# A new order of work between the set-up and the first feed-forward group of a two-layer S4 and SwiGLU network, the weights' high halves all cast on ScalarE, the norms' mean factor on GpSimd

## The chip, the core and the metric

One core of one Trainium2 chip runs the whole program. The metric is device time in microseconds (us), from the start of the execution to its end. The core has five instruction streams that each run strictly in order and wait for each other through semaphores: TensorE (PE in the profile), VectorE (DVE), ScalarE (ACT), GpSimd (POOL) and SyncE (SP, which here issues most of the DMAs).

## The reference

The input `u` is 1 x 2048 x 512 in fp32. Two layers follow one another, each an S4 convolution and a SwiGLU feed-forward step, both on a layer norm and both with a residual:

```python
def _A_ref(u, A_re, A_im, B_re, B_im, C_re, C_im, log_dt, Dskip):
    ...                                   # K: 512 kernels of length L, sums of 128 modes exp(dt*A*l)
    Yf = Uf * Kf[None, :, :, :]           # products of spectra, padded to 2L
    y = irfft(...)[..., :L]
    return y + u * Dskip
def _B_ref(x, w_gate, w_up, w_down):      # 512 -> 1376 -> 512
    return (_silu(x @ w_gate) * (x @ w_up)) @ w_down
x = A_u
for _ in range(2):                        # the same weights in both layers
    x = x + _A_ref(_layernorm(x), ...)
    x = x + _B_ref(_layernorm(x), w_gate, w_up, w_down)
```

## The kernel before, in words

**Blocks and groups.** The 2048 tokens are cut into four blocks of 512. Layer and block go in the order `SEQ` = (0,0), (0,1), (0,2), (1,0), (0,3), (1,1), (1,2), (1,3). A block first has its convolution (`ssm`, two halves of 256 channels, `ssm_half`) and then its feed-forward step in two groups of 256 tokens. The sixteen groups are counted here from 0, so group 2 is the first group of block (0,1) and group 4 the first of (0,2).

**The convolution** works on blocks of frequencies. In a half, four steps multiply the spectrum of the input by that of the kernel on VectorE (`yk`, a row of 128x1024 elements, L812, with `t` and L815 where there is an earlier block to add), take real and imaginary parts apart (L820, L821), and combine steps (L767, L768, L833 to L845). TensorE turns them back (`pi`, L784), and VectorE adds them to the residual (`xg` or `xf`, L793). The forward transform of the next input is `pf` on TensorE (L277).

**A feed-forward group** takes its layer norm in `ffn_norm`: `row_stats` sums rows on ScalarE (L223, L225, L226), GpSimd makes the inverse deviation by `pow` (L227), VectorE the factor of the mean (L228). Then, for each of two chunks of 128 tokens, ScalarE scales (L883) and casts to fp16 (L884), VectorE forms the low half `nn` (L885), and SyncE transposes both into `nhl2` (L887). TensorE then does `pgu`: a remainder of 48 small matmuls (L899 to L901; the first 24 read only the first chunk), and five turns of 48 (L930 to L933). Each turn ends in ScalarE's silu (`sg`, L936), VectorE's product (`sg`, L937), ScalarE's `hh` (L938) and VectorE's `hl` (L939). There are two buffers of `pgu` and two of `sg`. Last come 66 matmuls `py` (L946 to L948), and two VectorE rows (L953), one for each chunk, add them to the residual. The matmuls of a chunk end only with the last six of the 66.

**The set-up** makes the kernels' spectra in eight pieces ("lags", `pk`) and writes them out. **The transition** runs from the last lags to the first feed-forward group. There its order is written by hand for TensorE, VectorE, ScalarE and GpSimd, in generators advanced by `take(generator, n)`: `conv[0]` and `conv[1]` are the two halves of the first block, `first_parts` (L589, L590) completes the spectra `w0r` that the second half multiplies by, `odd` and `rest` are later spectra (`pw` L544 on TensorE, `wos` L607 and L608 on ScalarE, L609 on VectorE, a store by SyncE), `norm` is the first norm (statistics L207 to L213, `nn` L864, transposed on TensorE as `pt`, high half L869 on ScalarE, low half L871 on VectorE), `block1` the convolution of block (0,1), `last` a direct transform. `split(hi, lo, load)` takes the next steps of casting the weights to two fp16 halves: high halves of gate and up columns (ScalarE L675, the very first on VectorE L673), of w_down (ScalarE L700), low halves on VectorE (L680, L703), loads by SyncE (L668 for columns, L694 for w_down).

**After the transition** a list scheduler orders every engine with a timeline of its own, from the same program. Engines still run in the order so fixed.

Of the kernel before, what the change touches and what calls it, by code (L numbers as in the profile page):

```python
# [15 lines left out]
AF = mybir.ActivationFunctionType  # L16
OP = mybir.AluOpType
# [58 lines left out]
def kernel(ctx, tc, x, a_re, a_im, b_re, b_im, c_re, c_im, log_dt, d_skip,  # L76
# [139 lines left out]
    def row_stats(src, rows, scale, tag, junk):  # L216

        mv = tl([P, 4, 2], "mv", tag)
        rs = tl([P, 8], "rs", tag)
        nb = rs[:, 4:]  # L220
        c = 1.0 / (math.sqrt(D) * scale)
        for r in range(rows):
            A.activation(junk(r), src[:, r], AF.Identity, scale=-c / D, accum_out=mv[:, r, 0:1])  # L223
        for r in range(rows):
            A.activation(junk(r), src[:, r], AF.Square, scale=c, bias=mv[:, r, 0:1], accum_out=mv[:, r, 1:2])  # L225
        A.activation(mv[:, :rows, 1], mv[:, :rows, 1], AF.Identity, bias=epst[:, 0:1] if scale == 1.0 else epst[:, 1:2])  # L226
        G.tensor_tensor(rs[:, :rows], mv[:, :rows, 1], mhalf[:, :rows], OP.pow)  # L227
        V.scalar_tensor_tensor(nb[:, :rows], mv[:, :rows, 0], 1.0 / c, rs[:, :rows], OP.mult, OP.mult)  # L228
# [284 lines left out]
    def skip(ch, kt, eng):  # L513

        k = kt[0:1, :, 0]
        eng.tensor_tensor(k, k, dsk[:, ch * DC:(ch + 1) * DC].rearrange("p (g d) -> p g d", g=4), OP.add)
# [136 lines left out]
    def split_weights():  # L653


        cb = F // 4
        tags = iter(("bt", 0, 1, 2, "bt", 0, 1, 2, "n", "xf", "bt"))

        def columns(j, wi, src):
            fs = slice(j * cb, (j + 1) * cb)  # L660
            sc = sc6[:, wi:wi + 1]
            at = []

            def load():
                tag = next(tags)
                st = tl([P, 4, cb], "st2", tag) if isinstance(tag, str) else \
                    wsl[3].bitcast(F32)[:, 4 * cb * tag:4 * cb * (tag + 1)].rearrange("p (k f) -> p k f", k=4)
                nc.sync.dma_start(st, src[:, fs].rearrange("(k p) f -> p k f", p=P))  # L668
                at.append(st)

            def hi():
                if j == 0 and wi == 0:
                    V.tensor_scalar(wgu(wi, 0, 0, 4)[:, :, fs], at[0], sc, None, OP.mult)  # L673
                else:
                    A.activation(wgu(wi, 0, 0, 4)[:, :, fs], at[0], AF.Copy, scale=sc)  # L675

            def lo():
                n = 2 if wi == 0 else 4
                for k in range(0, 4, n):
                    V.scalar_tensor_tensor(wgu(wi, k, 1, n)[:, :, fs], at[0][:, k:k + n], sc,  # L680
                                           wgu(wi, 0, 0, 4)[:, k:k + n, fs], OP.mult, OP.subtract)
            return load, hi, lo

        def rows4(f0):
            n = min(4, F // P - f0)
            at = []

            def part(fc):
                rows = min(P, F - fc * P)
                sc = sc6[:rows, 2:3]  # L690

                def load():
                    st = tl([P, min(4, FT - f0), D], "st3", next(tags))
                    nc.sync.dma_start(st[:, :n], w_down[f0 * P:(f0 + n) * P].rearrange("(k p) d -> p k d", p=P))  # L694
                    if f0 + n < FT and n < 4:
                        nc.sync.dma_start(st[:F % P, n], w_down[(f0 + n) * P:])
                    at.append(st)

                def hi():
                    A.activation(wd(fc, 0)[:rows], at[0][:rows, fc - f0], AF.Copy, scale=sc)  # L700

                def lo():
                    V.scalar_tensor_tensor(wd(fc, 1)[:rows], at[0][:rows, fc - f0], sc, wd(fc, 0)[:rows],  # L703
                                           OP.mult, OP.subtract)
# [270 lines left out]
    with tc.manual_schedule(engines={mybir.EngineType.Activation, mybir.EngineType.DVE, mybir.EngineType.PE, mybir.EngineType.Pool}):  # L975
# [221 lines left out]
        take(tail["sp"], 2)  # L1197
        spread_pe(ks, kts[1])
        skip(c, kts[1], G)
        take(conv[0], 1)  # L1200
        while tops:
            tops.pop(0)()
        scales()
        split(1, 0)
        first_parts(c, 0)
        take(conv[0], 1)
        split(1, 1)
        split(0, 0, 1)
        first_parts(c, 2)
        split(1, 0)  # L1210
        take(conv[0], 1)
        first_parts(c - 1, 1)
        split(1, 0)
        take(last, 2)
        take(conv[1], 1)
        first_parts(c - 1, 3)
        take(conv[1], 1)
        split(0, 1)
        split(0, 0, 1)
        take(conv[0], 1)  # L1220
        take(conv[1], 1)
        split(1, 1)
        split(0, 0, 1)
        take(conv[1], 1)
        split(0, 1)
        split(0, 0, 1)
        take(odd, 2)
        take(conv[1], 1)
        direct_size()
        block1 = ssm(0, 1)  # L1230
        take(norm, 1)
        take(rest, 2)
        take(odd, 1)
        take(odd, 2)
        take(norm, 1)
        take(block1, 1)
        take(rest, 1)
        split(1, 0)
        take(odd, 1)
        take(norm, 1)  # L1240
        split(0, 1)
        take(rest, 3)
# [64 lines left out]
```

## Time and profile before

| | us |
|---|---|
| three runs: median (lowest to highest) | 1091.86 (1090.23 to 1092.86) |
| the profiled execution: its time, and its span | 1091.58, 1089.4 |
| PE busy in the span | 1026.5 (94%) |
| DVE busy | 969.3 (89%) |
| ACT busy | 547.4 (50%) |
| POOL busy | 109.6 (10%) |
| mean granted TensorE clock | 0.986 |

The time is the span and 2.2 us around it. Busy shares are means over stages with different limits, so the prediction reads them stage by stage. A row of the timeline gives the start, the length, engine, line and operation, the tile written and those read, and in brackets the idle time of the engine just before it and what ended it.

### The profile page before, as it was taken

Reading aid. Unit: us, or ns where it says so; the run is one execution under the profiler, and the core shown is the slowest. Engines: PE = TensorE matmul, PEld = TensorE weight load, DVE = VectorE, ACT = ScalarE, POOL = GpSimd, SP = SyncE. Lnnn points to the kernel's source line nnn. Section 1 sums busy time; section 2 is a strip of 40 time slices with the busy share of each in tenths; the row PEclk is TensorE's granted clock in tenths of the full one; section 3 lists DMA queues with packets and bytes.
Section 4 is the critical chain, followed back from the end, with each engine's and each line's share of the span. In section 5 each row is a group of like instructions: output and inputs, shape, how many; then the busy total and the mean of one; then the engine's idle time right before and its main releaser. Section 6 shows DMA issues by size and latency. Waiting matters only on the chain.

```text
span 1089.4 us, 22811 instructions
## 1 busy us (share of the span) xinstructions
PE 1026.5 (94%) x9302; PEld 810.9 (74%) x9302; DVE 969.3 (89%) x1405; ACT 547.4 (50%) x1093; POOL 109.6 (10%) x163
## 2 busy tenths in 40 slices
PE   1989999998779999999999999999999999999998
PEld 1868888887677777686779676786867687686775
DVE  8999999998999999999999989999998999993221
ACT  6989998953367162466462253533425432134211
POOL 1112222220002010012010001201100000000000
PEclk9989999998989999999999999999999999999999
DMA  5366777768765356342444553443545245312000
GB/s 212 108 180 167 173 166 179 187 181 272 234 182 172 120 145 215 105 141 68 131 117 133 158 160 130 119 136 100 166 126 180 59 127 147 109 61 63 2 25 20
DMA packets 125003, 149.23 MB, mean 137 GB/s; under 512 B 50897, under 2 KB 75985, under 8 KB 124130
## 3 DMA queue, kind: packets, MB, share of 16 engines
q1 hardware_dynamic: 112994, 122.27, 36.8%
q0 software_dynamic: 11904, 25.50, 10.0%
q8 instruction: 73, 1.20, 0.5%
q14 instruction: 32, 0.26, 0.1%
HBM read 97.66 MB, written 33.82 MB: 121 GB/s over the span
## 4 chain that ended last, share of the span: by engine, by line
PE 27%; DVE 27%; issue 11%; DMA 5%; ACT 3%; POOL 1%; SPq 0%; DVEq 0%; POOLq 0%; ACTq 0%
PE pgu L930 5%; PE pgu L931 5%; PE pgu L933 5%; DVE t L812 4%; DVE yk L815 4%; PE py L948 3%; PE py L946 3%; PE py L947 3%; DVE yk L812 3%; PE pi L784 2%; DVE sg L937 2%; DVE hl L939 2%; DMA n<-xdr 1%; DVE yl L232 1%; DMA mix<-nn 1%
## 5 line engine op out<-in xcount | busy, mean ns | idle before, releaser
L930 PE MATMUL pgu<-mix,wsl 128*128 128x256 f16 x1280 | 298.6, 273 | 5.4 <-DVE sg L937 2.1
L931 PE MATMUL pgu<-mix,wsl 128*128 128x256 f16 x1280 | 298.4, 273 | 0.0
L933 PE MATMUL pgu<-mix,wsl 128*128 128x256 f16 x1280 | 194.8, 273 | 0.0
L931 PEld LDWEIGHTS <-wsl 128*128 128x128 f16 x1280 | 125.2, 98 | 22.5 <-issue 6.7
L933 PEld LDWEIGHTS <-wsl 128*128 128x128 f16 x1280 | 125.2, 98 | 18.4 <-issue 3.8
L930 PEld LDWEIGHTS <-wsl 128*128 128x128 f16 x1280 | 125.2, 98 | 16.4 <-issue 1.2
L946 PE MATMUL py<-wsl,hh 128*128 128x512 f16 (+1 forms) x352 | 134.2, 381 | 0.1
L948 PE MATMUL py<-wsl,hl 128*128 128x512 f16 (+1 forms) x352 | 133.5, 381 | 0.1
L947 PE MATMUL py<-wsl,hh 128*128 128x512 f16 x320 | 121.8, 381 | 0.0
L815 DVE TENSOR_TENSOR yk<-yk,t 128x1024 f32<-128x1024 f32 x96 | 116.9, 1218 | 0.5
L812 DVE TENSOR_TENSOR t<-uu,w 128x1024 f32<-128x1024 f32 x96 | 117.0, 1218 | 0.3
L938 ACT ACTIVATE hh<-sg 128x512 f16<-128x512 f32 x80 | 50.1, 627 | 114.0 <-DVE sg L937 114.0
L544 PE MATMUL pw<-kt,ek 128*128 128x256 f32 (+1 forms) x384 | 93.2, 381 | 0.0
L937 DVE SCALAR_TENSOR_TENSOR sg<-pgu,sc,sg 128x512 f32<-128x512 f32 x80 | 59.6, 745 | 37.7 <-ACT sg L936 37.6
L936 ACT ACTIVATE sg<-pgu,sc 128x512 f32<-128x512 f32 x80 | 54.2, 678 | 70.7 <-PE pgu L933 66.9
L544 PEld LDWEIGHTS pw<-kt,ek 128*128 128x128 f32 x384 | 74.8, 199 | 8.8
L939 DVE TENSOR_TENSOR hl<-sg,hh 128x512 f16<-128x512 f32 x80 | 54.8, 685 | 15.3 <-ACT hh L938 15.3
L227 POOL TENSOR_TENSOR rs<-mv,mhalf 128x2 f32<-128x2 f32 (+1 forms) x21 | 33.6, 1598 | 336.3 <-ACT mv L226 296.3
L509 PE MATMUL pk<-re,g 128*32 128x64 f32 x1024 | 65.0, 317 | 2.2 <-DMA g<-g 1.9
L948 PEld LDWEIGHTS <-hl 128*128 128x128 f16 (+1 forms) x352 | 34.4, 98 | 39.2 <-issue 0.8
L947 PEld LDWEIGHTS <-hh 128*128 128x128 f16 (+1 forms) x352 | 34.6, 98 | 38.4 <-issue 0.8
L510 PE MATMUL pk<-im,g 128*32 128x64 f32 x1024 | 63.1, 301 | 0.0
(265 smaller groups left out, 2010.1 us busy)
## 6 DMA issues: line engine op xcount, KB each, us to landing
uu<-udr SPq DMA_DIRECT2D x96, 256.0 KB, 3.0
w<-wdr SPq DMA_DIRECT2D x96, 256.0 KB, 2.8
g<-g POOLq DMA_DIRECT2D x6, 1024.0 KB, 9.2
udr<-fu POOLq DMA_DIRECT2D x22, 256.0 KB, 2.7
udr<-u SPq DMA_DIRECT2D x16, 256.0 KB, 3.3
n<-xdr SPq DMA_DIRECT2D x4, 1024.0 KB, 6.4
kdr<-ks SPq DMA_DIRECT2D x6, 512.0 KB, 2.9
kt<-kdr SPq DMA_DIRECT2D x24, 128.0 KB, 3.0
```

The lines of the kernel that those rows point to most:

```text
L509: PE.matmul(o, lhsT=g[:, 0, :, d], rhs=re[:, 0:64, d], start=True, stop=False, tile_position=(0, 32 * grp))
L544: PE.matmul(pw[:, i], lhsT=e, rhs=kt[:, :, c + 4 * k0:4 * k1:4, :].rearrange("p g k d -> p k g d"), start=c == 0, stop=c == 3)
L812: V.tensor_tensor(t, uu.unsqueeze(2).to_broadcast([P, NQ, 2, 2, DC]), w.unsqueeze(3).to_broadcast([P, NQ, 2, 2, DC]), OP.mult)
L815: V.tensor_tensor(yk, yk, t, OP.add)
L930: PE.matmul(o, lhsT=wgu(wi, k, 0)[:, fs], rhs=nh[:, k], start=k == 0, stop=False)
L931: PE.matmul(o, lhsT=wgu(wi, k, 1)[:, fs], rhs=nh[:, k], start=False, stop=False)
L933: PE.matmul(o, lhsT=wgu(wi, k, 0)[:, fs], rhs=nlo[:, k], start=False, stop=k == 3)
L937: V.scalar_tensor_tensor(sg, pgu[:, 1], sc6[:, 4:5], sg, OP.mult, OP.mult)
L939: V.tensor_tensor(hl[:, f0:f0 + 2], sg, hh[:, f0:f0 + 2], OP.subtract)
L946: PE.matmul(py[r], lhsT=hh[:n, f, rc], rhs=wd(f, 0)[:n], start=f == 0, stop=False)
L947: PE.matmul(py[r], lhsT=hh[:n, f, rc], rhs=wd(f, 1)[:n], start=False, stop=False)
L948: PE.matmul(py[r], lhsT=hl[:n, f, rc], rhs=wd(f, 0)[:n], start=False, stop=f == FT - 1)
```

## The change

Three edits. In `row_stats` the mean's factor (a product of two columns, 128x2 or 128x4, 21 times in the program) moves from VectorE to GpSimd, behind `pow` on the same engine, and the scale of the sums moves into the small Identity. The first high half of the weights is cast by ScalarE as the others are. And the steps of the transition stand in a new order: `conv[0]` runs ahead of the tail of the spectra, the four `first_parts` stand together behind the first half's inverse transforms, `conv[1]` follows earlier, the first norm stands directly behind it, the products of `block1` leave the transition for the scheduled part behind it, low halves of the weights stand where these were, and `direct_size` and `sizes` come last. Two lines are removed by it, so later lines have other numbers: 812 is 810, 784 is 782, 680 is 678, 703 is 701, 885 is 883, 937 is 935, 953 is 951; lines of the spectra are one up (609 is 610), and the product on GpSimd is L229.

```diff
-        c = 1.0 / (math.sqrt(D) * scale)
+        c = 1.0 / (D * scale ** 2)
         for r in range(rows):
-            A.activation(junk(r), src[:, r], AF.Identity, scale=-c / D, accum_out=mv[:, r, 0:1])
+            A.activation(junk(r), src[:, r], AF.Identity, scale=-1.0 / D, accum_out=mv[:, r, 0:1])
...
-        V.scalar_tensor_tensor(nb[:, :rows], mv[:, :rows, 0], 1.0 / c, rs[:, :rows], OP.mult, OP.mult)
+        G.tensor_tensor(nb[:, :rows], mv[:, :rows, 0], rs[:, :rows], OP.mult)
...
             def hi():
-                if j == 0 and wi == 0:
-                    V.tensor_scalar(wgu(wi, 0, 0, 4)[:, :, fs], at[0], sc, None, OP.mult)
-                else:
-                    A.activation(wgu(wi, 0, 0, 4)[:, :, fs], at[0], AF.Copy, scale=sc)
+                A.activation(wgu(wi, 0, 0, 4)[:, :, fs], at[0], AF.Copy, scale=sc)
...
+        take(conv[0], 1)
         first_parts(c, 0)
...
+        first_parts(c - 1, 3)
+        take(conv[1], 1)
...
-        direct_size()
-        block1 = ssm(0, 1)
-        take(norm, 1)
-        take(rest, 2)
...
-        take(block1, 1)
...
+        block1 = ssm(0, 1)
...
+        direct_size()
+        sizes(c, kts[1], ks)
```

**VectorE from the end of the first block's convolution to the low half of the first norm.** `wsl` are weights, `st` a loaded piece of them, `xg` the residual, `bb` and `yk` the convolution, `t`, `u`, `uu` the products of block (0,1), `wos` and `mix<-pw` later spectra, and `mix<-pt` is the first norm's low half. Before, with the convolution of block (0,1) between the norm's statistics and its low half:

```order
L207 BN_STATS st<-xg 128x6
L208 BN_AGGR mv<-st 128x2
L207 BN_STATS st<-xg 128x6
L208 BN_AGGR mv<-st 128x2
L209 TENSOR_SCALAR rs<-mv 128x2
L680 SCALAR_TENSOR_TENSOR wsl_2661<-st_2740,sc_92,wsl_2661 128x2x344
L680 SCALAR_TENSOR_TENSOR wsl_2662<-st_2740,sc_92,wsl_2661 128x2x344
L213 SCALAR_TENSOR_TENSOR rs<-mv,rs 128x2
L609 TENSOR_TENSOR wos<-pw,wos 128x2x3x64
L812 TENSOR_TENSOR yk<-u,w0r 128x1024
L812 TENSOR_TENSOR t<-uu,w 128x1024
L815 TENSOR_TENSOR yk<-yk,t 128x1024
```
...
```order
L767 TENSOR_TENSOR mix<-bb,mix 128x512
L812 TENSOR_TENSOR yk<-u,w0r 128x1024
L609 TENSOR_TENSOR wos<-pw,wos 128x2x3x64
L768 TENSOR_TENSOR bb<-bb,mix 128x512
L609 TENSOR_TENSOR mix<-pw,mix 128x2x3x64
L871 TENSOR_TENSOR mix<-pt,mix 128x1024
```

After, from the same place:

```order
L207 BN_STATS st<-xg 128x6
L208 BN_AGGR mv<-st 128x2
L207 BN_STATS st<-xg 128x6
L208 BN_AGGR mv<-st 128x2
L209 TENSOR_SCALAR rs<-mv 128x2
L678 SCALAR_TENSOR_TENSOR wsl_2663<-wsl_2664,sc_92,wsl_2662 128x4x344
L213 SCALAR_TENSOR_TENSOR rs<-mv,rs 128x2
L701 SCALAR_TENSOR_TENSOR wsl_2663<-st_2935,sc_92,wsl_2663 128x512 x2
L610 TENSOR_TENSOR wos<-pw,wos 128x2x3x64
L869 TENSOR_TENSOR mix<-pt,mix 128x1024
```

What moved: the products of block (0,1) are gone from behind the statistics (L213), and the norm's low half (L869) stands three rows behind them instead of nineteen. Of w_down's low halves (L701) two stand directly behind the statistics.

**VectorE at the norm of group 2.** `nn` (L885 before, L883 after) is the low half of a norm's chunk, two for each norm; `sg` is the product of a `pgu` turn. Before, the last turn ahead of the second `nn` and that `nn`:

```order
L937 SCALAR_TENSOR_TENSOR sg_3034<-pgu,sc_92,sg_3034 128x512
L232 SCALAR_TENSOR_TENSOR fu<-pf,fu 128x512
L635 TENSOR_SCALAR sy<-sy 128x2
L767 TENSOR_TENSOR bb<-bb 128x512
L812 TENSOR_TENSOR yk<-fbt,w0r 128x1024
L885 TENSOR_TENSOR nn_3010<-nn_3010 128x512
```

After, from the last `sg` that stands ahead of the second `nn` (this is the last turn of group 1, the tenth in all):

```order
L935 SCALAR_TENSOR_TENSOR sg_3021<-pgu,sc_92,sg_3021 128x512
L791 TENSOR_TENSOR xg<-xg,pi 128x2x256
L818 TENSOR_TENSOR bb<-yk 128x256
L819 TENSOR_TENSOR bb<-yk 128x256
L810 TENSOR_TENSOR t<-uu,w 128x1024
L937 TENSOR_TENSOR hl<-sg_3021,hh 128x512
L810 TENSOR_TENSOR yk<-fu,w0r 128x1024
L791 TENSOR_TENSOR xg<-xg,pi 128x2x256
L813 TENSOR_TENSOR yk<-yk,t 128x1024
L631 TENSOR_SCALAR sy<-pm 128x1
L810 TENSOR_TENSOR t<-uu,w 128x1024
L632 TENSOR_SCALAR sy<-sy 128x1
```

These twelve rows follow directly:

```order
L883 TENSOR_TENSOR nn_2997<-nn_2997 128x512
L813 TENSOR_TENSOR yk<-yk,t 128x1024
L633 TENSOR_SCALAR sy<-sy 128x1
L818 TENSOR_TENSOR bb<-yk 128x256
L634 TENSOR_SCALAR sy<-sy 128x1
L819 TENSOR_TENSOR bb<-yk 128x256
L810 TENSOR_TENSOR t<-uu,w 128x1024
L635 TENSOR_SCALAR sy<-sy 128x1
L765 TENSOR_TENSOR bb<-bb 128x512
L810 TENSOR_TENSOR yk<-fbt,w0r 128x1024
L233 SCALAR_TENSOR_TENSOR fbt<-pf,fu 128x512
L883 TENSOR_TENSOR nn_2997<-nn_2997 128x512
```

What moved: before, the eighth `sg` of the program is the last one ahead of this norm, with four rows between them; now it is the tenth, with 22 rows between.

**VectorE at the norm of group 4.** `xg<-py` is the end of a group, `xf` the residual of block (0,2), `fbt` and `fu` its forward spectra. Before, from the first `nn` to the second:

```order
L885 TENSOR_TENSOR nn_3010<-nn_3010 128x512
L841 TENSOR_TENSOR bb<-bb 128x512
L232 SCALAR_TENSOR_TENSOR yl_4065<-bb,sy,yl_4065 128x512
L844 TENSOR_TENSOR mix<-mix 128x256
L845 TENSOR_TENSOR mix<-mix 128x256
L939 TENSOR_TENSOR hl<-sg_3034,hh 128x512
L232 SCALAR_TENSOR_TENSOR yl_4065<-bb,sy,yl_4065 128x512
L232 SCALAR_TENSOR_TENSOR fu<-pf,fbt 128x512
L232 SCALAR_TENSOR_TENSOR z_3035<-n,z_3035 128x1024
L885 TENSOR_TENSOR nn_3010<-nn_3010 128x512
```

After, the end of the same norm (the other `xg<-py` of the pair stands four rows ahead of the first row here):

```order
L233 SCALAR_TENSOR_TENSOR xf<-pi,sy,xf 128x2x256
L883 TENSOR_TENSOR nn_2997<-nn_2997 128x512
L766 TENSOR_TENSOR mix<-mix,bb 128x512
L831 TENSOR_TENSOR bb<-bb 128x512
L951 SCALAR_TENSOR_TENSOR xg<-py,sc_92,xg 128x512
L233 SCALAR_TENSOR_TENSOR fbt<-pf,fbt 128x512
L834 TENSOR_TENSOR bb<-mix 128x256
L835 TENSOR_TENSOR bb<-mix 128x256
L839 TENSOR_TENSOR bb<-bb 128x512
L883 TENSOR_TENSOR nn_2997<-nn_2997 128x512
```

What moved: before, both rows `xg<-py` of group 3 stand 26 rows behind the second `nn`; now they stand ahead of it, and the first of them ahead of the first `nn`. On TensorE, group 4's remainder stands behind the last `py` of group 3 in both orders. After, between the last six `py`, which are that chunk pair's end, stand six `pf` and eleven `pi` (ahead of the very last one), then twelve `pf`, then the remainder.

More of the change, by code (lines that the diff above doesn't have):

```diff
@@ L1196 @@
         take(conv[0], 1)
-        take(tail["sp"], 2)
+        take(conv[0], 1)
         spread_pe(ks, kts[1])
         skip(c, kts[1], G)
+        take(tail["sp"], 2)
         take(conv[0], 1)
@@ L1203 @@
         scales()
-        split(1, 0)
+        take(conv[0], 1)
         first_parts(c, 0)
-        take(conv[0], 1)
-        split(1, 1)
-        split(0, 0, 1)
         first_parts(c, 2)
         split(1, 0)
+        first_parts(c - 1, 1)
+        first_parts(c - 1, 3)
+        take(conv[1], 1)
         take(conv[0], 1)
-        first_parts(c - 1, 1)
+        take(conv[1], 1)
+        split(0, 1)
+        split(0, 0, 1)
+        take(conv[1], 1)
         split(1, 0)
@@ L1215 @@
         take(conv[1], 1)
-        first_parts(c - 1, 3)
+        split(1, 0)
         take(conv[1], 1)
+        take(norm, 1)
+        split(0, 0, 1)
+        take(odd, 2)
+        take(rest, 2)
+        take(norm, 1)
+        split(1, 0)
+        take(odd, 1)
+        take(norm, 1)
+        ready = nhl2[:, 0, 0], nhl2[:, 0, 1]
+        block1 = ssm(0, 1)
         split(0, 1)
         split(0, 0, 1)
[L1220 to L1224, printed above, removed]
+        take(rest, 1)
         split(0, 1)
@@ L1227 @@
         take(odd, 2)
-        take(conv[1], 1)
-        direct_size()
-        block1 = ssm(0, 1)
-        take(norm, 1)
         take(rest, 2)
+        split(1, 1)
+        split(0, 0, 1)
         take(odd, 1)
-        take(odd, 2)
-        take(norm, 1)
-        take(block1, 1)
         take(rest, 1)
[L1238 to L1242, printed above, removed]
+        take(rest, 2)
+        split(1, 1)
         take(conv[0], 1)
         take(conv[1], 1)
-        ready = nhl2[:, 0, 0], nhl2[:, 0, 1]
+        take(rest, 1)
+        take(rest, 2)
         split(1, 1)
-        take(rest, 3)
+        take(rest, 1)
+        direct_size()
+        sizes(c, kts[1], ks)
+        split(0, 0, 2)
         split(1, 1)
-        take(rest, 4)
-        split(0, 0, 3)
-        sizes(c, kts[1], ks)
         nn2 = tl([P, 2, D], "nn2", "nn")
```

5 lines of the change are left out of this document (3 added, 2 removed).

## Prediction

> **What bounds the kernel now.** I read the windows by stage first, then TensorE's rows at the first feed-forward turns, then the waits, and last the rows at the later norms. The windows give, for each stretch, the busy time of TensorE, its weight loads, VectorE, ScalarE and GpSimd, then the granted clock:
>
> ```profile
> core 0: us, PE busy (x) PEld busy (x) DVE busy (x) ACT busy (x) POOL busy (x), PEclk, DMA share, GB/s
> 246.00:345.00 99.00, 81.93 (x736) 71.98 (x735) 92.08 (x149) 52.31 (x102) 9.05 (x4) 0.91 0.71 226
> 345.00:506.00 161.00, 158.46 (x1345) 121.76 (x1343) 157.21 (x246) 74.75 (x150) 13.95 (x22) 1.00 0.44 131
> 506.00:1000.00 494.00, 484.05 (x4004) 365.51 (x4003) 461.61 (x668) 200.41 (x384) 33.19 (x44) 1.00 0.42 123
> ```
>
> In the transition TensorE is idle for 99 - 81.93 = 17.1 us; behind it, up to 1000, for 2.5 + 10.0 us. VectorE is full in both first stretches: its idle time is 6.9 us in 99 and 3.8 in 161. So the transition can give something, and what it gives is kept only if TensorE then finds its work ready in time.
>
> ```profile
> 300.46 0.27 PE L930 MATMUL pgu<-mix,wsl 128*128 128x256 f16 x1 [1.11 <-ACT mix L869]
> 327.95 0.75 DVE L937 SCALAR_TENSOR_TENSOR sg<-pgu,sc,sg 128x512 f32<-128x512 f32 x1
> 328.75 0.27 PE L930 MATMUL pgu<-mix,wsl 128*128 128x256 f16 x1 [1.90 <-DVE sy L623]
> 350.37 0.27 PE L930 MATMUL pgu<-mix,wsl 128*128 128x256 f16 x1
> ```
>
> The first turn starts at 300.46. The third, at 328.75, waits for the first `sg` of VectorE at 327.95, since it writes the buffer which that row reads. The fifth starts at 350.37, 21.6 us later.
>
> **The transition, new order.** Clock times of the changed kernel are sums of durations of before.
>
> ```profile
> 250.45 0.97 DVE L572 TENSOR_TENSOR wo<-pw,wo 128x768 f32<-128x768 f32 x1 [2.31 <-ACT w0r L568]
> 257.09 0.94 DVE L673 TENSOR_SCALAR wsl<-st,sc 128x1376 f16<-128x1376 f32 x1
> 259.88 1.77 DVE L680 SCALAR_TENSOR_TENSOR wsl<-st,sc,wsl 128x688 f16<-128x688 f32 x2
> 261.88 0.66 PE L589 MATMUL pw<-kt,ef 128*128 128x64 f32 x4 [1.79 <-POOL kt L516]
> 264.13 0.28 ACT L590 ACTIVATE w0r<-pw 128x128 f32<-128x128 f32 x1 [2.96 <-PE pw L589]
> 266.35 1.22 DVE L812 TENSOR_TENSOR yk<-mix,w0r 128x1024 f32<-128x1024 f32 x1
> ```
>
> The wait of 2.31 is filled by convolution rows, the high half (0.94, 0.85 from start to start) goes to ScalarE, which sat idle for 2.96 there, and the pair of low halves (1.69 from start to start) goes behind. So VectorE comes to the second half's first product (266.35) at 266.35 - 2.31 - 0.85 - 1.69 = 261.5. It needs `first_parts`, which now stand behind four inverse matmuls that wait for that same moment: `pw` at 262.5 to 263.7 and `w0r` some 2.5 us later, as in the rows: 265 to 266.2. I take 265.8: VectorE idles 4.3 (3.5 to 4.7), and starts the second half only 0.5 us earlier. In it two big low halves go (start to start 4.8 us less the pair put there, 1.7), `dmax` goes (0.6), one early product comes (1.1), and one wait for the inverse grows by 0.5: the statistics stand at 288.85 - 0.5 - 3.1 - 0.6 + 1.1 + 0.5 = 286.2.
>
> ```profile
> 288.85 0.67 DVE L207 BATCH_NORM_STATS2 st<-xg 128x6 f32<-128x512 f32 x1
> 289.41 1.89 PE L784 MATMUL pi<-bb,mix 128*128 128x256 f32 x8
> 291.33 1.54 SPq L694 DMA_DIRECT2D st<-in_B_w_down_dram  x2
> 292.34 0.15 DVE L213 SCALAR_TENSOR_TENSOR rs<-mv,rs 128x2 f32<-128x2 f32 x1
> 296.60 1.95 ACT L700 ACTIVATE wsl<-st,sc 128x512 f16<-128x512 f32 x3 [2.56 <-DMA st<-in_B_w_down_dram]
> 297.36 1.41 DVE L703 SCALAR_TENSOR_TENSOR wsl<-st,sc,wsl 128x512 f16<-128x512 f32 x2 [0.88 <-ACT wsl L700]
> 299.39 1.02 ACT L869 ACTIVATE mix<-pt 128x1024 f16<-128x1024 f32 x1 [0.84 <-PE pt L866]
> 295.63 5.30 SPq L810 DMA_DIRECT2D uu<-udr  x2
> 301.29 1.45 ACT L675 ACTIVATE wsl<-wsl,sc 128x1376 f16<-128x1376 f32 x1
> 308.09 1.21 DVE L871 TENSOR_TENSOR mix<-pt,mix 128x1024 f16<-128x1024 f32 x1
> ```
>
> Statistics to L213 take 3.5 as before: 289.7. Next in line are w_down's low halves. Its load started when the last inverses ended (289.41 + 1.89) and took 5.25 to ScalarE's first cast; the inverses now end at about 287.6, with the later spectra behind them, so the cast starts at 292.9 and VectorE goes on at 293.7: 4.0 idle (2.3 to 4.6). Two low halves bring it to 295.0. The next row, `wos`, needs ScalarE, which has in its list three casts (1.95), the norm's high half (1.02), a column cast (1.45) and four small copies (1.0): 292.9 + 5.4 = 298.3, and 3.3 more are idle. The norm's low half ends at 299.9, against 309.3 before. On SyncE's queue the loads of block (0,1), such as `uu` (5.30 for two, from 295.63), move behind this load and the stores of the later spectra; the products that read them moved too, so I price that at nothing; if they came late, VectorE's convolution rows at 314 would wait.
>
> From there to the first `sg` the list holds 17.6 us of rows, and a ping-pong of `wos` copies leaves about 2 idle (1 to 2.5): first `sg` at 319.4, third turn at 320.2 instead of 328.75. **The lead is 8.5 us at that point.** VectorE idles for it 4.3 + 4.0 + 3.3 + 2.0, and 1.5 at the inverse: 15.1.
>
> Up to the fifth turn TensorE's list now holds 96 turn matmuls, 24 `py` and a remainder: 96 x 0.109 + 24 x 0.216 + 48 x 0.041 = 17.6 us, by the steps given below. With equal work the fifth turn of before would be at 350.37 - (21.6 - 17.6) = 346.4. But ScalarE has 17.9 us of rows between the first silu (318.7) and the fourth, whose buffer the fifth turn waits for, and waits in it for GpSimd:
>
> ```profile
> 337.60 4.44 POOL L227 TENSOR_TENSOR rs<-mv,mhalf 128x2 f32<-128x2 f32 x1 [3.64 <-ACT mv L226]
> 337.94 2.92 ACT L255 ACTIVATE n<-n,rs 128x512 f32<-128x512 f32 x4
> L227 POOL TENSOR_TENSOR rs<-mv,mhalf x21: 695/1269/4438, 331.2 to 993.8; 128x2 f32<-128x2 f32 x15, 128x4 f32<-128x4 f32 x6
> L228 DVE SCALAR_TENSOR_TENSOR rs<-mv,rs x21: 143/160/165, 334.4 to 994.6; 128x2 f32<-128x2 f32 x15, 128x4 f32<-128x4 f32 x6
> ```
>
> No row shows the product on GpSimd. Bounds are its `pow` of the same size, 0.70 to 4.44, against 0.16 on VectorE; I take 1.3, the median; the other twenty products stand at norms that, but for those below, are done long before they are read. Pow and product are 2.6, partly beside ScalarE's other rows. Fifth turn: 318.7 + 17.9 + 2.6 + the silu's and the turn's start (about 1.1) = 340.3. **The lead is 346.4 - 340.3 = 6.1 us**, between 3.5 (a slow product) and 8.5 (no wait).
>
> **What takes it back.** Before, the remainders of groups 2 and 4 (415.44 and 517.93) follow `py` without a gap; group 2's last transpose was issued at 397.03:
>
> ```profile
> 397.03 1.19 SPq L887 DMA_TRANSPOSE mix<-nn  x1
> 415.44 0.21 PE L899 MATMUL pgu<-wsl,mix 128*128 128x96 f16 x1
> 517.72 0.38 PE L948 MATMUL py<-wsl,hl 96*128 96x512 f16 x1
> 517.93 0.21 PE L899 MATMUL pgu<-wsl,mix 128*128 128x96 f16 x1
> mix<-nn SPq DMA_TRANSPOSE x60, 2.5
> 382.31 1.22 DVE L812 TENSOR_TENSOR t<-uu,w 128x1024 f32<-128x1024 f32 x1
> 383.45 1.22 DVE L812 TENSOR_TENSOR yk<-fu,w0r 128x1024 f32<-128x1024 f32 x1
> 384.58 0.68 DVE L793 TENSOR_TENSOR xg<-xg,pi 128x512 f32<-128x512 f32 x1
> 385.18 0.15 DVE L630 TENSOR_SCALAR sy<-pm 128x1 f32<-128x1 f32 x1
> 386.67 1.47 PE L277 MATMUL pf<-z,eh 128*128 128x256 f16 x12
> 501.81 0.82 PE L784 MATMUL pi<-yl,mix 128*128 128x256 f16 x6
> ```
>
> A transpose lands in 2.5 us; the rows give steps of 1.14 for 1024 elements, 0.60 for 512, 0.33 for 256 (half of it, an estimate), 0.07 for small ones, and on TensorE 0.216 for `py`, 0.109 for `pf` and `pi` in fp16 (twelve in 1.47 with the last one's full length). A turn's matmul has the same 256 columns, so the same step; a remainder's has 96, an estimate of 0.041.
>
> Group 2: the second `nn` stands 22 rows behind the last turn's `sg` of group 1. From that turn's end it takes 0.8 (silu), then seven rows of 1024, eight of 512, four of 256 and five small ones, 14.6, then 2.5: 17.9. TensorE has left 54 `py`, twelve `pf`, six `pi` of 0.22 (fp32) and half a remainder, with six `pf`: 11.7 + 1.3 + 1.3 + 1.7 = 16.0. It waits 1.9 (1 to 3.5).
>
> Group 4: both ends of group 3 stand ahead of the second `nn`. Counted from the third-last `py` of the first chunk's end, the first `nn` lands after 0.4 + 3.2 + 2.5 = 6.1; TensorE has left three `py`, eighteen `pf` and eleven `pi`, 4.0, and waits 2.1. The second lands after 6.1 + 4.4 = 10.5 against 4.0 + 2.1 + 1.7 = 7.8: 2.7 more. Together 4.8 (4 to 7). It holds whatever the lead, as both sides hang on TensorE itself. VectorE's extra idle time, 15.1 less 6.9 in this stage before, and some 3 where GpSimd holds up ScalarE, makes group 2's norm about 11 late. By that count its transposes land at 397.03 + 2.5 + 11 = 410.5, while TensorE, 6.1 ahead, would want the second half at 415.44 - 6.1 + 1.0 = 410.3. That is the same moment within the terms' bounds, so it doesn't add.
>
> Sum against the profiled 1091.58: - 6.1 + 1.9 + 4.8 = + 0.6: 1092.2, 0.3 above the median 1091.86. A measurement of this kernel can tell about 0.2% (2.2 us) from no change, so the forecast is no change.
>
> **Rivals.** *Faster (0.30):* the waits for GpSimd behind 345 go as well.
>
> ```profile
> DVE rs L228 <- POOL rs L227: 9.8, 9, 3.3
> ```
>
> VectorE no longer stands for these 9.8 us, and TensorE idles 10.0 from 506 to 1000. If the lead stays at 8.5 and a third of those 10 go, it is 1092.2 - 2.4 - 3.3 = 1086.5. Against it: behind 506 norms mostly have slack, and 9.8 is nearly all in VectorE's idle time, not TensorE's. It decides from some 2 us of gaps saved.
>
> *Slower (0.32):* the product on GpSimd costs as much as the slowest `pow`, 4.4 instead of 1.3, at the first norms, where VectorE is full: the lead is 3.1 smaller, 1095.3. The spread 0.70 to 4.44 for one size speaks for it; the median speaks against. It decides from a product of 3.5 us. The Trainium skill (page "SBUF — State Buffer", section "SBUF: two separate sides") says that VectorE and GpSimd share a port pair as an exclusive lock, which the one that starts first holds for its whole instruction while the other fully blocks. By that rule a product waits for VectorE's running row at most: with 1.22 for that row and 0.70 for itself it takes 1.9, and the sum would be 1092.8. The trace has a `pow` of 4.44 where no VectorE row is longer than 1.4, so it agrees with a wait, not with that bound.
>
> *No change (0.38)* is the sum above, 1090 to 1094 by the bounds of its terms.
>
> The range takes the faster rival's end and some 2 above the slower one's, for a wait of 7 at group 4: 1086 to 1097.
>
> **What would show it.** Right: first `sg` near 319, the third turn near 320, the fifth near 340; gaps of TensorE ahead of the remainders of groups 2 and 4, of about 2 and 5 us, ended by transposes; VectorE idle ahead of the second half's first product, of w_down's low halves and of the first `wos`. Wrong: no gap at group 4, a product on GpSimd over 3 us, or fewer gaps behind 506.

## The result and the profile after

The changed kernel takes 1100.69 us, median of four runs (1097.78 to 1101.82), against 1091.38 for the kernel before on the same chip (1090.23 to 1092.86). The ratio is 1.0079 with a 95% interval of 1.0065 to 1.0094: slower, and outside the predicted range of 1086 to 1097. The profiled execution has a span of 1100.0 us, 10.6 more than the one before. Of these, 8.2 are idle time of TensorE (71.1 us in the whole span against 62.9), and 2.4 are a longer busy time for the same 9302 matmuls (1028.9 against 1026.5), at a mean granted clock of 0.983 against 0.986. One execution of e5_vprod, a kernel described below, took 3673 us and counts in none of its figures.

The windows of the changed kernel, with the stretches and columns of the prediction's first view:

```profile
core 0: us, PE busy (x) PEld busy (x) DVE busy (x) ACT busy (x) POOL busy (x), PEclk, DMA share, GB/s
246.00:345.00 99.00, 83.64 (x799) 71.81 (x798) 79.65 (x129) 55.20 (x108) 7.50 (x7) 0.92 0.68 209
345.00:506.00 161.00, 159.85 (x1280) 119.70 (x1279) 156.80 (x238) 66.12 (x134) 17.40 (x25) 1.00 0.46 139
506.00:1000.00 494.00, 474.24 (x3955) 363.31 (x3954) 467.59 (x669) 195.68 (x371) 38.56 (x56) 0.99 0.41 123
```

TensorE's idle time is 15.4 us in the transition (17.1 before), 1.2 in the next stretch (2.5) and 19.8 from 506 to 1000 (10.0 before). Most of the loss is in the last stretch, far behind the hand-written order.

The ends of the groups, each the end of a second row `xg<-py` of VectorE, show when it comes. Group 4 ends at 574.8 us in both kernels, with nearly the same number of matmuls done (5122, and 5136 before). At the end of group 7 the changed kernel is 5.0 us behind, at the end of group 10 it is 9.8 behind, and at the last group's end 10.6.

The transition itself went as worked out. TensorE's third and fifth turns and the VectorE rows that release them, from the timeline of the changed kernel:

```profile
320.08 0.75 DVE L935 SCALAR_TENSOR_TENSOR sg<-pgu,sc,sg 128x512 f32<-128x512 f32 x1 [0.16 <-ACT sg L934]
320.89 0.27 PE L928 MATMUL pgu<-mix,wsl 128*128 128x256 f16 x1 [1.07 <-DVE sg L935]
335.98 2.10 POOL L229 TENSOR_TENSOR rs<-mv,rs 128x4 f32<-128x4 f32 x1
340.95 0.75 DVE L935 SCALAR_TENSOR_TENSOR sg<-pgu,sc,sg 128x512 f32<-128x512 f32 x1 [2.92 <-ACT sg L934]
341.75 0.27 PE L928 MATMUL pgu<-mix,wsl 128*128 128x256 f16 x1 [2.64 <-DVE sg L935]
264.72 1.23 DVE L810 TENSOR_TENSOR yk<-mix,w0r 128x1024 f32<-128x1024 f32 x1 [3.46 <-ACT w0r L591]
292.63 0.75 DVE L701 SCALAR_TENSOR_TENSOR wsl<-st,sc,wsl 128x512 f16<-128x512 f32 x1 [2.96 <-ACT wsl L698]
297.07 0.56 DVE L610 TENSOR_TENSOR wos<-pw,wos 128x384 f32<-128x384 f32 x1 [3.03 <-ACT wos L609]
```

The three waits of VectorE that the prediction named (the last three rows) are there, at the rows it named, each within 1.1 us.

What goes wrong later shows best at one norm of layer 1. This is the timeline of the changed kernel there: ScalarE first, then GpSimd, then the TensorE row that waited.

```profile
836.69 0.67 ACT L934 ACTIVATE sg<-pgu,sc 128x512 f32<-128x512 f32 x1
837.26 0.29 ACT L226 ACTIVATE mv<-mv,epst 128x4 f32<-128x4 f32 x1
843.22 2.93 ACT L256 ACTIVATE n<-n,rs 128x512 f32<-128x512 f32 x4 [5.67 <-POOL rs L229]
846.05 0.61 ACT L936 ACTIVATE hh<-sg 128x512 f16<-128x512 f32 x1
846.57 0.67 ACT L934 ACTIVATE sg<-pgu,sc 128x512 f32<-128x512 f32 x1
847.14 1.04 ACT L268 ACTIVATE z<-n 128x1024 f16<-128x1024 f32 x1
837.64 1.58 POOL L228 TENSOR_TENSOR rs<-mv,mhalf 128x4 f32<-128x4 f32 x1 [26.87 <-ACT mv L226]
839.29 3.90 POOL L229 TENSOR_TENSOR rs<-mv,rs 128x4 f32<-128x4 f32 x1
848.24 0.58 PE L278 MATMUL pf<-z,eh 128*128 128x256 f16 x2 [5.00 <-ACT z L268]
```

Directly behind the norm's sums (837.26) stands the row that needs the factor (843.22). ScalarE waits 5.67 us for GpSimd, and in its queue behind it stand a turn's `hh`, the next silu and `z`, which TensorE then waits 5.00 us for. Summed over the span from 345 to 1010, the waits of ScalarE for a norm's factor are, before and after (us in total, times, longest):

```profile
ACT nn L883 <- DVE rs L228: 15.8, 11, 3.2
ACT n L255 <- DVE rs L228: 1.0, 2, 0.7
```

```profile
ACT nn L881 <- POOL rs L229: 19.4, 12, 3.2
ACT n L256 <- POOL rs L229: 17.3, 5, 5.7
```

So 16.8 us became 36.7.

### The profile page after: what moved, and what is told of

The parts are those of the page before. It is cut to its first block, busy times and chain, and to the rows that moved or that the text cites. A ratio compares the mean times of both kernels' runs of the same rounds, so it can differ in the third digit from the quotient of the medians.

```text
span 1100.0 us, 22817 instructions
## 1 busy us (share of the span) xinstructions
PE 1028.9 (94%) x9302; PEld 810.9 (74%) x9302; DVE 966.3 (88%) x1383; ACT 548.3 (50%) x1094; POOL 118.2 (11%) x184
## 3 DMA queue, kind: packets, MB, share of 16 engines
q0 software_dynamic: 11904, 25.50, 10.2%
## 4 chain that ended last, share of the span: by engine, by line
PE 34%; DVE 23%; ACT 7%; DMA 5%; issue 4%; POOL 2%; SPq 0%; DVEq 0%; ACTq 0%; POOLq 0%
PE pgu L931 6%; PE pgu L928 6%; PE pgu L929 6%; DVE t L810 4%; DVE yk L813 3%; PE py L944 3%; PE py L946 3%; PE py L945 3%; DMA mix<-nn 2%; DVE yk L810 2%; PE pi L782 2%; DVE sg L935 1%; DVE hl L937 1%; DVE yl L233 1%; PE pf L278 1%
## 5 line engine op out<-in xcount | busy, mean ns | idle before, releaser
L928 PE MATMUL pgu<-mix,wsl 128*128 128x256 f16 x1280 | 302.9, 275 | 9.5 <-DVE sg L935 4.4
L929 PE MATMUL pgu<-mix,wsl 128*128 128x256 f16 x1280 | 302.8, 275 | 0.0
L931 PE MATMUL pgu<-mix,wsl 128*128 128x256 f16 x1280 | 197.5, 275 | 0.0
L929 PEld LDWEIGHTS <-wsl 128*128 128x128 f16 x1280 | 126.3, 99 | 27.3 <-issue 10.6
L510 PE MATMUL pk<-re,g 128*32 128x64 f32 x1024 | 65.2, 317 | 3.2 <-DMA g<-g 2.2
L511 PE MATMUL pk<-im,g 128*32 128x64 f32 x1024 | 63.2, 302 | 0.0
L944 PEld LDWEIGHTS <-hh 128*128 128x128 f16 (+1 forms) x352 | 34.5, 98 | 38.2 <-ACT hh L936 0.5
L945 PEld LDWEIGHTS <-hh 128*128 128x128 f16 (+1 forms) x352 | 34.5, 98 | 37.7
## 6 DMA issues: line engine op xcount, KB each, us to landing
g<-g POOLq DMA_DIRECT2D x6, 1024.0 KB, 9.0
n<-xdr SPq DMA_DIRECT2D x4, 1024.0 KB, 5.9
```

The lines of the kernel that those rows point to most:

```text
L510: PE.matmul(o, lhsT=g[:, 0, :, d], rhs=re[:, 0:64, d], start=True, stop=False, tile_position=(0, 32 * grp))
L928: PE.matmul(o, lhsT=wgu(wi, k, 0)[:, fs], rhs=nh[:, k], start=k == 0, stop=False)
L929: PE.matmul(o, lhsT=wgu(wi, k, 1)[:, fs], rhs=nh[:, k], start=False, stop=False)
L931: PE.matmul(o, lhsT=wgu(wi, k, 0)[:, fs], rhs=nlo[:, k], start=False, stop=k == 3)
L944: PE.matmul(py[r], lhsT=hh[:n, f, rc], rhs=wd(f, 0)[:n], start=f == 0, stop=False)
L945: PE.matmul(py[r], lhsT=hh[:n, f, rc], rhs=wd(f, 1)[:n], start=False, stop=False)
```

## The experiments

Three theories were on the table after the result. *Product:* the factor on GpSimd costs the time. *Order:* the new transition makes VectorE late and group 4 stalls, and the rest follows. *Scheduler:* any edit reshuffles the rows behind the transition and moves the time by several us. The first four kernels split the change into its parts. Medians are compared with the kernel before as it ran in the same batch (1092.0, 1092.7 and 1092.3).

### The product alone, in the old order (e1_prod)

```diff
-        V.scalar_tensor_tensor(nb[:, :rows], mv[:, :rows, 0], 1.0 / c, rs[:, :rows], OP.mult, OP.mult)
+        G.tensor_tensor(nb[:, :rows], mv[:, :rows, 0], rs[:, :rows], OP.mult)
```
(with the scale of the sums moved, as in the change)

> The kernel before with one edit alone: the mean's factor (the product) on GpSimd behind pow, sums scaled as in the changed kernel. Product theory (a product on GpSimd is held up while VectorE runs rows back to back, ScalarE stands behind it, and TensorE's inputs come late): 1096 to 1100, with ScalarE's waits for GpSimd's product over 25 us in all and at least one TensorE gap of 3 us or more behind such a wait. Order theory (the loss comes from the new transition: VectorE is late behind it and the ends of group 3 stand ahead of group 4's norm): 1090 to 1093.

Measured: 1102.17, ratio 1.0108 (1.0079 to 1.0137), 2 us above the range of the product theory. The product alone costs at least as much as the whole change. The expected single gap of 3 us isn't there: the longest of TensorE's gaps between 345 and 1010 us is 2.3 us. ScalarE's waits for the factor, 37.9 us, and the stretch 506 to 1000 of this kernel:

```profile
ACT nn L884 <- POOL rs L229: 32.3, 13, 5.4
ACT n L256 <- POOL rs L229: 5.6, 4, 1.9
```

```profile
506.00:1000.00 494.00, 477.13 (x3982) 362.97 (x3980) 463.31 (x657) 196.28 (x379) 45.66 (x57) 1.00 0.41 123
```

### The change without the product (e2_order)

```diff
-        G.tensor_tensor(nb[:, :rows], mv[:, :rows, 0], rs[:, :rows], OP.mult)
+        V.scalar_tensor_tensor(nb[:, :rows], mv[:, :rows, 0], 1.0 / c, rs[:, :rows], OP.mult, OP.mult)
```

> The changed kernel with the product back on VectorE and the sums scaled as before; the new transition and the first high half on ScalarE stay. Product theory: the lead of 4.7 us at the fifth turn survives but for some 2 to 4 us at group 4, so 1088 to 1091. Order theory: 1097 to 1101, with the gaps ahead of group 4's remainder (about 7 us in the changed kernel) and again at group 8.

Measured: 1087.14, ratio 0.9961 (0.9946 to 0.9976): faster than both kernels. The order theory falls, since the new order is all there. TensorE's idle time from 506 to 1000 is back at 10.2 us, and ScalarE's waits are 20.9:

```profile
506.00:1000.00 494.00, 483.80 (x4059) 369.65 (x4059) 469.35 (x684) 203.30 (x391) 30.71 (x44) 0.99 0.41 124
```

```profile
ACT nn L880 <- DVE rs L228: 16.2, 12, 3.4
ACT n L255 <- DVE rs L228: 4.7, 3, 2.0
```

The same norm as above, in this kernel's timeline, ScalarE, GpSimd, VectorE:

```profile
833.45 0.29 ACT L226 ACTIVATE mv<-mv,epst 128x4 f32<-128x4 f32 x1
834.37 0.63 ACT L935 ACTIVATE hh<-sg 128x512 f16<-128x512 f32 x1 [0.63 <-DVE sg L934]
834.90 0.67 ACT L933 ACTIVATE sg<-pgu,sc 128x512 f32<-128x512 f32 x1
835.57 2.93 ACT L255 ACTIVATE n<-n,rs 128x512 f32<-128x512 f32 x4
833.82 1.02 POOL L227 TENSOR_TENSOR rs<-mv,mhalf 128x4 f32<-128x4 f32 x1 [35.85 <-ACT mv L226]
835.38 0.15 DVE L228 SCALAR_TENSOR_TENSOR rs<-mv,rs 128x4 f32<-128x4 f32 x1
```

Here `hh` and the silu stand ahead of the row that needs the factor, and that row doesn't wait at all. This is the reading that the later experiments test.

### The first high half on ScalarE alone, in the old order (e3_hi)

```diff
-                    V.tensor_scalar(wgu(wi, 0, 0, 4)[:, :, fs], at[0], sc, None, OP.mult)
+                    A.activation(wgu(wi, 0, 0, 4)[:, :, fs], at[0], AF.Copy, scale=sc)
```

> The kernel before with one edit alone: the first high half of the weights cast by ScalarE instead of VectorE. Product theory and order theory: 1090 to 1093, since ScalarE was idle there and VectorE gains 0.85 us. Scheduler theory (any edit makes the list scheduler place the rows behind the transition anew, and that alone moves the time by several us): off from 1091.4 by 3 us or more, in either direction.

Measured: 1088.76, ratio 0.9974 (0.9961 to 0.9986), a gain of 3.3 us where one row of 0.85 us was freed. That is about the bound of 3 us that the scheduler theory had set (the result is 3.3 us under the kernel before in its batch, 2.6 under the 1091.4 that the theory named), so the theory may have a part in it. But three kernels with the product on VectorE lie from 1087 to 1092, and those without from 1100 to 1102: reshuffling alone doesn't bridge that.

### The product on ScalarE, in the new order (e4_act)

```diff
-        G.tensor_tensor(nb[:, :rows], mv[:, :rows, 0], rs[:, :rows], OP.mult)
+        for r in range(rows):
+            A.activation(nb[:, r:r + 1], mv[:, r, 0:1], AF.Copy, scale=rs[:, r:r + 1])
```

> The changed kernel with the product on ScalarE, one small row per chunk (two or four per norm, about 0.2 us each from start to start), so GpSimd has pow alone as before. Product theory: 1088 to 1092, as GpSimd no longer works twice behind VectorE's rows. Order theory: 1097 to 1101.

Measured: 1101.29, ratio 1.0089 (1.0070 to 1.0108). This kills the product theory as it stood: GpSimd runs only `pow`, and the time is the same. So far, it is leaving VectorE that costs, wherever the product goes. (ScalarE has 54 small rows more here; e11_acthop below has them too and is 10 us faster, so they aren't the cause.) ScalarE waits 27.9 us for `pow`, and TensorE is idle for 23.4 us in the last stretch:

```profile
ACT rs L230 <- POOL rs L228: 27.9, 18, 4.7
```

```profile
506.00:1000.00 494.00, 470.61 (x3944) 361.08 (x3944) 467.35 (x668) 202.92 (x414) 36.99 (x43) 0.99 0.42 123
```

That left three readings. *Distance:* the scheduler decides how many ScalarE rows stand between the norm's sums (L226) and the first row that needs the factor. With the factor passing through VectorE's full queue it leaves many; without, it puts the consumer directly behind, and the chip's `pow` is slower than that allows. *Yield:* VectorE's own wait for `pow` leaves GpSimd undisturbed. *Latency:* the factor is simply later. The built orders give the distance, summed over the 21 norms: 32 rows in the kernel before, 38 in e2_order, 40 in e3_hi, against 18 in the changed kernel, 27 in e1_prod and 16 in e4_act. Counted in the traces, they come out within two rows of these. The new scaling of the sums went along with every slow kernel so far, so it needed a control too.

### The new sums with the product on VectorE (e5_vprod)

```diff
-        G.tensor_tensor(nb[:, :rows], mv[:, :rows, 0], rs[:, :rows], OP.mult)
+        V.tensor_tensor(nb[:, :rows], mv[:, :rows, 0], rs[:, :rows], OP.mult)
```

> The changed kernel with the product on VectorE as a plain product; the sums keep the new scaling, the transition its new order. If the new scaling of the sums cost the time: 1099 to 1102. If it is only where the product stands: 1086 to 1089, as with product and sums of before.

Measured: 1087.44, the median of three executions, ratio 0.9947 (0.9929 to 0.9966). The scaling costs nothing.

### The product on GpSimd, copied by VectorE (e6_hop)

```diff
-        G.tensor_tensor(nb[:, :rows], mv[:, :rows, 0], rs[:, :rows], OP.mult)
+        G.tensor_tensor(rs[:, 8:8 + rows], mv[:, :rows, 0], rs[:, :rows], OP.mult)
+        V.tensor_scalar(nb[:, :rows], rs[:, 8:8 + rows], 1.0, None, OP.mult)
```

> The changed kernel, product on GpSimd, and its result copied by one small VectorE row that ScalarE's scaling waits for. The factor comes later than in the changed kernel, but the scheduler now leaves 38 ScalarE rows between the norms' last sums and the scaling, where the changed kernel leaves 18 and the one before 32. Distance theory (ScalarE stands idle behind GpSimd, because the scheduler puts the scaling directly behind the sums): 1086 to 1091. Latency theory (the factor is late on GpSimd): 1100 to 1104. Yield theory (VectorE's wait leaves the port to GpSimd): 1086 to 1091.

Measured: 1094.65, ratio 1.0021 (1.0010 to 1.0033). A further step on the factor's way makes the kernel 6 us faster than the changed one. Latency alone can't do that. It is 3.7 us above the upper end that distance and yield gave. And the profile shows the gain only in part: ScalarE's waits for the factor fall from 36.7 to 21.0 + 4.1 = 25.1 us, but TensorE's idle time from 506 to 1000 is 19.3 us, as in the changed kernel (19.8):

```profile
506.00:1000.00 494.00, 474.70 (x3968) 362.74 (x3968) 468.24 (x681) 199.79 (x382) 40.46 (x56) 1.00 0.42 123
```

In the whole span TensorE is idle for 68.8 us, against 71.1. The rest of the gain is a busy time of 1024.0 us instead of 1028.9, at a granted clock of 0.989 instead of 0.983.

### A VectorE row that waits for pow and serves nobody (e7_dummy)

```diff
+        V.scalar_tensor_tensor(rs[:, 8:8 + rows], mv[:, :rows, 0], 1.0, rs[:, :rows], OP.mult, OP.mult)
         G.tensor_tensor(nb[:, :rows], mv[:, :rows, 0], rs[:, :rows], OP.mult)
```

> The changed kernel with one more VectorE row per norm, a product of before's form that waits for pow and whose result nobody reads; ScalarE still takes the factor from GpSimd, with 22 rows of distance. Yield theory: 1086 to 1091, as VectorE waits for pow again. Distance theory and latency theory: 1098 to 1103.

Measured: 1101.12, ratio 1.0074 (1.0057 to 1.0091). VectorE waits for `pow` again, and GpSimd does get shorter rows by it: the median product takes 0.21 us instead of 0.40, the longest 2.12 instead of 3.90. The time is the same, so the yield theory doesn't explain the loss.

```profile
L230 POOL TENSOR_TENSOR rs<-mv,rs x21: 194/211/2123, 328.8 to 1012.2; 128x2 f32<-128x2 f32 x15, 128x4 f32<-128x4 f32 x6
```

A gain of a few us isn't ruled out: this kernel ends group 0 4.2 us later than the changed one, and has made that up by the last group. TensorE's idle time from 506 to 1000 is still 17.4 us:

```profile
506.00:1000.00 494.00, 476.57 (x3979) 364.62 (x3978) 473.61 (x689) 200.73 (x388) 36.42 (x57) 0.99 0.41 123
```

### The product on ScalarE, behind a VectorE copy (e11_acthop)

```diff
+        V.tensor_scalar(rs[:, 8:8 + rows], rs[:, :rows], 1.0, None, OP.mult)
         for r in range(rows):
-            A.activation(nb[:, r:r + 1], mv[:, r, 0:1], AF.Copy, scale=rs[:, r:r + 1])
+            A.activation(nb[:, r:r + 1], mv[:, r, 0:1], AF.Copy, scale=rs[:, 8 + r:9 + r])
```
(against e4_act)

> The changed kernel with the product on ScalarE, but reading a copy of the deviations that one small VectorE row makes. The scheduler leaves 37 ScalarE rows between the norms' last sums and the first row that needs the factor, where the same product without the copy had 16 and took 1101.3. Distance theory: 1086 to 1092. Latency theory (each further step on the way of the factor costs): 1101 to 1105.

Measured: 1091.29, ratio 0.9984 (0.9968 to 1.0001), 10 us less than e4_act, which does the same without the copy. ScalarE waits 19.8 us and TensorE is idle for 10.7 in the stretch, against 27.9 and 23.4 in e4_act (the profiled execution took 1088.6 us, 2.7 under the median):

```profile
ACT rs L231 <- DVE rs L229: 19.8, 17, 2.3
```

```profile
506.00:1000.00 494.00, 483.28 (x4050) 368.93 (x4049) 471.41 (x686) 210.96 (x426) 32.60 (x44) 0.99 0.42 125
```

### The new order alone (e14_ord)

```diff
+                if j == 0 and wi == 0:
+                    V.tensor_scalar(wgu(wi, 0, 0, 4)[:, :, fs], at[0], sc, None, OP.mult)
+                else:
+                    A.activation(wgu(wi, 0, 0, 4)[:, :, fs], at[0], AF.Copy, scale=sc)
```
(against e2_order)

> The new order of the transition alone: product and sums as before, first high half on VectorE. If the order is worth its lead of some 5 to 8 us less the stall at group 4: 1087 to 1090. If the first high half on ScalarE brought the gain (alone it gave 1088.8): 1091 to 1094.

Measured: 1087.43, ratio 0.9961 (0.9946 to 0.9976). The order is worth 4.9 us by itself; the first high half adds nothing to it, though it gave 3.3 in the old order.

### The old order, product on GpSimd, copied by VectorE (e16_hop_b)

The edit of e6_hop, in e1_prod.

> The kernel before with product on GpSimd, its result copied by a small VectorE row; 38 ScalarE rows of distance, where product on GpSimd alone had 27 and took 1102.2, and the kernel before has 32. Distance theory: 1091 to 1096, with what a slow product on GpSimd still costs. Latency theory: 1102 to 1106.

Measured: 1094.69, ratio 1.0023 (1.0011 to 1.0035), 7.5 us less than e1_prod.

All of it in one table:

| order | product | distance, rows | norms with no row | TensorE idle in the span, us | us |
|---|---|---|---|---|---|
| old | VectorE (before) | 32 | 6 | 62.9 | 1091.4 to 1092.7 |
| old, first high half on ScalarE (e3) | VectorE | 40 | 2 | 63.2 | 1088.8 |
| new, first high half on VectorE (e14) | VectorE | 38 | 4 | 59.5 | 1087.4 |
| new (e2) | VectorE | 38 | 4 | 60.5 | 1087.1 |
| new, new sums (e5) | VectorE | 38 | 4 | - | 1087.4 |
| new (e11) | ScalarE, copy on VectorE | 37 | 3 | 61.1 | 1091.3 |
| new (e6) | GpSimd, copy on VectorE | 38 | 4 | 68.8 | 1094.7 |
| old (e16) | GpSimd, copy on VectorE | 38 | 5 | 65.2 | 1094.7 |
| old (e1) | GpSimd | 27 | 10 | 72.3 | 1102.2 |
| new (e7) | GpSimd, idle VectorE row | 22 | 10 | 71.5 | 1101.1 |
| new (the change) | GpSimd | 18 | 12 | 71.1 | 1100.7 |
| new (e4) | ScalarE | 16 | 12 | 73.2 | 1101.3 |

The fourth column is counted in the traces: at how many of the 21 norms the first row that needs the factor stands directly behind the sums. The fifth is the span less PE's busy time on the first lines of each page.

Every kernel with 32 rows or more stays under 1095, every one with 27 or fewer is above 1100, in both orders. Three pairs differ only by the copy on VectorE, with the product on the same engine: the one with the copy is 10.0, 6.0 and 7.5 us faster. So it isn't the time of the product on its engine that makes most of the loss, but that no VectorE row stands on the factor's way to ScalarE; and each time it is then that the scheduler sets ScalarE's row closer behind the sums. Shorter rows of GpSimd alone gained nothing (e7_dummy).

That the close order of ScalarE itself does it, and not that of another engine, is argued from the norm shown above and from this table. The copy moves rows on all engines, and no run moved ScalarE's rows alone. Nor do the sizes follow the measures: e1_prod has only five rows fewer than the kernel before and costs 10 us (the norms without a row tell the two apart better, 10 against 6), and ScalarE waits 25.1 us for the factor in e6_hop and 20.7 + 4.8 = 25.5 in e7_dummy, which are 6.5 us apart.

The engine counts as well. At about the same distance in the new order, the product costs some 4 us more on ScalarE (e11_acthop) and some 7 more on GpSimd (e6_hop) than on VectorE.

## Why the prediction was wrong

**Right: the transition.** First `sg` was given as 319.4 and came at 320.08, the third turn as 320.2 and came at 320.89, the waits of 4.3, 4.0 and 3.3 as 3.46, 2.96 and 3.03. The fifth turn came at 341.75 for 340.3: the product took 2.10 there for the 1.3 assumed. The lead by equal work is 346.4 - 341.75 = 4.7 us, inside 3.5 to 8.5. One thing wasn't counted: after the gap of 2.64 us the next stretch ran at a granted clock of 0.60.

```profile
341.70:346.00 4.30, 4.25 (x24) 3.17 (x24) 4.30 (x6) 3.44 (x6) 0.20 (x1) 0.60 0.36 95
```

That is an estimate of 4.3 x 0.4 = 1.7 us more.

**Right in kind, and in size partly by luck: group 4.** From the timeline of the changed kernel, the second end of group 3 ahead of the second `nn`, and TensorE's waits there:

```profile
509.63 1.47 PE L278 MATMUL pf<-z,eh 128*128 128x256 f16 x12 [1.80 <-ACT fbt L279]
511.61 0.22 PE L897 MATMUL pgu<-wsl,mix 128*128 128x96 f16 x1 [0.51 <-DMA mix<-nn]
512.91 0.22 PE L899 MATMUL pgu<-wsl,mix 128*128 128x96 f16 x1 [0.32 <-DMA mix<-nn]
514.84 0.22 PE L897 MATMUL pgu<-wsl,mix 128*128 128x96 f16 x1 [0.82 <-DMA mix<-nn]
519.79 0.22 PE L899 MATMUL pgu<-wsl,mix 128*128 128x96 f16 x1 [2.89 <-DMA mix<-nn]
510.97 0.74 DVE L951 SCALAR_TENSOR_TENSOR xg<-py,sc,xg 128x512 f32<-128x512 f32 x1
513.50 0.68 DVE L883 TENSOR_TENSOR nn<-nn 128x512 f16<-128x512 f32 x1
514.19 0.34 SPq L237 DMA_DIRECT2D xg<-in_A_u_dram  x1
514.62 1.20 SPq L885 DMA_TRANSPOSE mix<-nn  x1
```

Waits ended by transposes are 0.51 + 0.32 + 0.82 + 2.89 = 4.5 us, for 4.8 predicted; a wait of 1.80 for ScalarE's `fbt` comes on top. But the last transpose, issued at 514.62 right behind a load of 1024 KB, landed 5.1 us later instead of 2.5. Landing in 2.5, it would have been there at 517.1, and TensorE, which had finished its other work at 516.9, would have waited 0.2 instead of 2.89: 1.9 in all, an estimate. In e2_order the transposes make TensorE wait 1.71 there. **Group 2** was predicted to wait 1.9 and did not, as far as the trace tells since TensorE came there with less lead; in e2_order, with more, it waited 1.46.

**The sum so far.** The terms up to group 4 gave + 0.6, and at the end of group 4 the two kernels are level. That nearness is partly luck: a smaller lead (4.7 us for 6.1) and the lower clock (1.7 us that weren't counted) are nearly made up by the wait at group 2 that didn't come (1.9), and at group 4 a late transpose made up the size. The 10.6 us that separate the spans come behind it, where the sum has no term.

**Wrong: the product's term.** This is the step that failed. The prediction priced the product by its own duration at one norm (1.3 us) and the other twenty at nothing, since their norms "are done long before they are read". That holds for TensorE's remainders: outside group 4 no wait of TensorE between 345 and 1010 us is ended by a transpose of `nn`. It leaves out ScalarE's queue, where the row that waits for the factor holds up silus, casts and inputs of the transforms behind it, as at the norm shown above. And it left out that the product's place changes the order there: ahead of the prediction the orders of VectorE and TensorE are compared, and ScalarE's isn't. Measured, the product off VectorE costs 1100.7 - 1087.1 = 13.6 us in the new order and 1102.2 - 1092.0 = 10.2 in the old one. Without that term the sum would have been 1092.2 - 1.3 = 1090.9 or a little less, against 1087.1 measured for e2_order; the lead there is larger, since the fifth turn doesn't wait.

**The rivals.** The slower one had the right edit and side, but the wrong place: it priced one slow product at the first norm (1095.3), where the product took 2.10 us, not the 3.5 it asked for. One of the prediction's signs of being wrong, a product on GpSimd over 3 us, did come, but at a later norm (3.90 at 839.29). The faster one rested on VectorE's 9.8 us of waits for GpSimd. They did go, and ScalarE's waits grew by twice as much, from 16.8 to 36.7, with TensorE's inputs queued behind them.

**Open.** Why the first high half alone gives 3.3 us in the old order and nothing in the new one isn't settled; a reshuffle by the scheduler would do it, but no run separates that. Where the 13.6 us arise is known only in steps: the changed kernel is 5.3 us behind e2_order at the end of group 4, 11.0 at group 7, 15.3 at group 10 and 15.0 at the end. Which norm carries how much isn't shown, nor why the changed kernel runs at a lower granted clock than e6_hop. The fastest versions here are the change without the product (1087.1, 0.4% under the kernel before and 1.2% under the changed one) and the two beside it in the table, which can't be told from it.

## What to carry to other kernels

When a small row is moved to another engine, look at what stands behind its consumer in the consumer's queue, and compare that queue's order before and after, not only those of the engines that lose or gain the row. A small row on a full engine can be worth keeping where an automatic scheduler, because of it, puts other work ahead of the consumer; here three pairs of kernels point that way. And a change of several edits is best split at once: here two edits together gained 5 us and the third lost 10 to 14.

## What the runs showed of the hardware

The duration of a tiny product on GpSimd depends on VectorE's rows beside it. In the changed kernel it spans a factor of twenty:

```profile
L229 POOL TENSOR_TENSOR rs<-mv,rs x21: 195/403/3895, 326.8 to 1015.5; 128x2 f32<-128x2 f32 x15, 128x4 f32<-128x4 f32 x6
```

The longest, 839.29 to 843.19, lies over four VectorE rows with both inputs in SBUF that follow one another without a gap, and ends 0.07 us after the last of them:

```profile
839.57 1.22 DVE L810 TENSOR_TENSOR t<-uu,w 128x1024 f32<-128x1024 f32 x1
840.71 0.68 DVE L765 TENSOR_TENSOR bb<-bb 128x512 f32<-128x512 f32 x1
841.31 1.22 DVE L810 TENSOR_TENSOR yk<-fbt,w0r 128x1024 f32<-128x1024 f32 x1
842.44 0.68 DVE L766 TENSOR_TENSOR bb<-bb 128x512 f32<-128x512 f32 x1
```

VectorE rows that read TensorE's output (`pgu`, `pi`) didn't hold it up in two cases: the product at 891.10 took 0.20 us under this row, and so did the one at 591.29 under a row `sg<-pgu`.

```profile
891.03 0.74 DVE L233 SCALAR_TENSOR_TENSOR xg<-pi,sy,xg 128x512 f32<-128x512 f32 x1
```

The Trainium skill (page "SBUF — State Buffer", section "SBUF: two separate sides") has a VectorE row with two SBUF inputs and a GpSimd row that reads SBUF lock a shared port pair against each other for a whole instruction. The trace agrees with the lock, and goes further than the prediction's bound of one row of 1.22: 3.90 us over four rows here, and up to 6.83 us in e1_prod. In these cases GpSimd didn't get its turn between rows that follow closely. The profile's spans on GpSimd are rough, so the ends are less sure than the order.
